# Linear attention and a SiLU feed-forward: reordered loads, split exps and a later transpose around batch 1 of 8

## The chip, the cores and the metric

The kernel runs on one core of a Trainium2 chip. A core has five engines with queues of their own, each working in program order: PE (TensorE, matmuls and transposes), DVE (VectorE), ACT (ScalarE), POOL (GpSimd) and SP (SyncE, which here only issues transfers). Sixteen DMA engines move data between the main memory (HBM) and the on-chip memory (SBUF); matmul results stand in PSUM, eight banks in all. The metric is the device time of one execution in microseconds (us); lower is better.

## The reference

Attention without a softmax over pairs of rows, then a feed-forward layer, in float32:

```python
# q, k, v: (8 batches, 8 heads, 576 rows, 64)
q_s = exp(q - max(q, -1)); q_s /= sum(q_s, -1) + 1e-9
k_s = exp(k - max(k, 2));  k_s /= sum(k_s, 2) + 1e-9
kv   = einsum('bhsd,bhse->bhde', k_s, v)
attn = einsum('bhsd,bhde->bhse', q_s, kv)
# x: (4608 tokens, 512), heads side by side
h = x @ w_in                 # 512 -> 2048
out = (h * sigmoid(h)) @ w_out   # 2048 -> 512
```

## The kernel before

There are two tilings at once. The attention goes by batch b (8 of 576 rows), the feed-forward by chunk t (9 of 512 tokens); a chunk's tokens come from one or two batches. Chunk 0 is done 576 wide, so that it takes the whole of batch 0.

For a batch, q, k and v are loaded in two halves of four heads each (`load`, index cc; two buffers of each name, so a load waits until the same half of the batch before has been read). `exp_q` and `exp_k` run on ACT. The row sums of q come from `qsum` (DVE) or, for batch 1, from `qsum_pair` (two additions on POOL) and `qsum_end` (DVE); `qnorm` divides. `tr` transposes q on PE and `trcopy` brings it out of PSUM (batches 0 and 1), or `q_transpose` does both by a DMA (later batches). `vcast` rounds v to bf16 in the one buffer `vaug`, which has a column of constants beside v, `kv_both` multiplies k and v on PE (72 small matmuls, and `kvcopy` on DVE, which divides by the sums of k), and `xt` makes the chunk's input XT.

The feed-forward of the later chunks is done with Winograd's form of Strassen's method: seven products in place of eight, over sums and differences of blocks. `ws_op`, `xs_op`, `t_op` and `s_op` make those sums on DVE, all from SBUF to SBUF: WS from W1, XS from XT, T1 to T4 from W2, and S from the activations. `group` is a product of the first layer with its evacuation (`group_snap`, `group_add`, `group_silu`), `prod` one of the second. Chunk 0 uses plain matmuls: `wide` (first layer, 16 units, each with a tanh on ACT and a product on DVE, in three pairs of PSUM banks in turn) and `mm2_plain` (second layer).

The order is written out by hand. `units` is the list of PE's pieces of work; `plan(u, f)` issues f just before unit u, and functions with the same u go out in the order of the plans. Each engine does what it is given in that order, so a plan sets an instruction's place in the queues of ACT, DVE, POOL and SP, and not a time. `b1 = begin[1]` is 16, the first unit after the wide ones: nine units of `mm2_plain`, then fourteen that alternate `group` of chunk 1 with `mm2_plain`, then eight plain units of chunk 1; `begin[2]` is 47.

What the change touches: the issue order of the loads on POOL's queue ahead of the main loop (lines 561 to 573); the plans at units 9 to 13 for batch 1's exps and sums; `tr(1, 1, ...)` and its `trcopy` (lines 777 and 779); `ws_op(1, 0)` (line 801); and batch 3's six loads, issued by SP among the stores of chunk 0 (`mm2_plain_out` ends in `store`, two transfers on SP's queue).

Of the kernel before, what the change touches and what calls it, by code (L numbers as in the profile page):

```python
# [17 lines left out]
def kernel(  # L18
# [9 lines left out]
    nc = tc.nc  # L28
# [4 lines left out]
    J = S // P  # L33
# [53 lines left out]
    def copy(eng, o, i):  # L87
        if eng is nc.scalar:
            eng.copy(out=o, in_=i)  # L89
        else:  # L90
            eng.tensor_copy(o, i)  # L91

    def load(b, name, src, cc, eng):
        t = ld.tile([128, 2, J * D], FP32, name=name)
        st[b][name, cc] = t
        x = src[b].rearrange("(g r) (p j) d -> g (r p) (j d)", r=2, j=J)
        eng.dma_start(out=t, in_=x.rearrange("g x y -> x g y")[:, 2 * cc:2 * cc + 2, :])  # L97

    def jgd(b, name, cc):
        return st[b][name, cc].rearrange("p g (j d) -> p j g d", d=D)  # L100

    def half(t, cc):
        return t[:, :, cc * 128:(cc + 1) * 128].rearrange("p j (g d) -> p j g d", d=D)

    def exp_q(b, cc, g0=0, g1=2):
        if "eq" not in st[b]:
            st[b]["eq"] = ap.tile([128, J, NG * D], BF16, name="eq")
        nc.scalar.activation(  # L108
            out=half(st[b]["eq"], cc)[:, :, g0:g1], in_=jgd(b, "qt", cc)[:, :, g0:g1], func=ACT.Exp
        )  # L110
# [4 lines left out]
    def vcast(b, cc, eng, g0=0, g1=2):  # L115
        o = vaug[:, :, 2 * cc + g0:2 * cc + g1, 0:D]
        i = jgd(b, "vt", cc)[:, :, g0:g1, :]
        copy(eng, o, i)

    def qsum_pair(b, cc):  # L120
        e = half(st[b]["eq"], cc)
        t1 = mp.tile([128, 2 * TCH], FP32, name="h0", bufs=1)[:, 0:J * D]
        t1 = t1.rearrange("p (j g d) -> p j g d", g=2, d=D // 2)
        t2 = mp.tile([128, 2 * TCH], FP32, name=f"h{cc + 1}", bufs=1)[:, 0:J * D // 2]
        t2 = t2.rearrange("p (j g d) -> p j g d", g=2, d=D // 4)
        nc.gpsimd.tensor_tensor(
            out=t1, in0=e[:, :, :, 0:D // 2], in1=e[:, :, :, D // 2:D], op=ALU.add
        )
        nc.gpsimd.tensor_tensor(
            out=t2, in0=t1[:, :, :, 0:D // 4], in1=t1[:, :, :, D // 4:D // 2], op=ALU.add  # L130
        )
        st[b]["t2", cc] = t2

    def qsum_end(b, cc):
        new_zq(b)
        nc.vector.reduce_sum(out=st[b]["zq"][:, cc], in_=st[b]["t2", cc], axis=AX.X)
        nc.vector.reciprocal(out=st[b]["rzq"][:, cc], in_=st[b]["zq"][:, cc])
# [16 lines left out]
    def qnorm(b, cc, eng):  # L154
        e = half(st[b]["eq"], cc)
        r = st[b]["rzq"][:, cc]
        eng.tensor_tensor(  # L157
            out=e, in0=e, in1=r[:, :, :, None].to_broadcast([128, J, 2, D]), op=ALU.mult
        )

    def new_qt(b):
        if "qT" not in st[b]:
            st[b]["qT"] = ap.tile([128, J, 2, 128], BF16, name="qT", bufs=2)
        return st[b]["qT"]
# [7 lines left out]
    def tr(b, cc, j0, j1, bank):  # L172
        t = PS[:, bank, :].bitcast(BF16)
        for j in range(j0, j1):
            nc.tensor.transpose(
                out=t[:, (j - j0) * 128:(j - j0 + 1) * 128],
                in_=st[b]["eq"][:, j, cc * 128:(cc + 1) * 128],
                identity=ident,
            )

    def trcopy(b, cc, j0, j1, bank, eng=nc.vector):
        t = PS[:, bank, :].bitcast(BF16)[:, 0:(j1 - j0) * 128].rearrange("x (j y) -> x j y", y=128)
        copy(eng, new_qt(b)[:, j0:j1, cc, :], t)
# [25 lines left out]
    def kv_both(b):  # L209
        kv(b, 0)  # L210
        kv(b, 1)
        kvcopy(b)
# [92 lines left out]
    def wa(c, f):  # L305
        return W1[:, 2 * c:2 * c + 2, f * 128:(f + 4) * 128]
# [4 lines left out]
    def ws_op(i, g):  # L311
        w, f0, f1 = WS[g], 4 * g + 8, 4 * g
        in0, in1, op = {
            1: (wa(0, f1), wa(1, f1), ALU.add),
            2: (w[0], wa(0, f0), ALU.subtract),
            3: (wa(0, f0), wa(0, f1), ALU.subtract),
            4: (wa(1, f0), w[1], ALU.subtract),
        }[i]
        nc.vector.tensor_tensor(out=w[i - 1], in0=in0, in1=in1, op=op)
# [30 lines left out]
    def group_silu(t, i, f, n):  # L350
        x = group_bank(t, False) if i is None else four(t, i)
        nc.scalar.activation(out=group_out(t, f, n), in_=x, func=ACT.Silu, scale=1.0 / XS)  # L352
# [46 lines left out]
    def store(t, col, o):  # L399
        for i in range(2):  # L400
            nc.sync.dma_start(out=rows(t, col + i * P), in_=o[i * P:(i + 1) * P, :])
# [11 lines left out]
    def mm2_plain_out(t, m, eng):  # L413
        if m % 2 == 0:
            st[t]["ow"] = mp.tile([128, 2, DM], FP32, name="ow", bufs=3)
        o = st[t]["ow"][:, m % 2]
        if eng is nc.scalar:
            nc.scalar.activation(out=o, in_=PS[:, 2 + m], func=ACT.Copy, scale=OS)
        else:
            nc.vector.tensor_scalar_mul(out=o, in0=PS[:, 2 + m], scalar1=OS)  # L420
        store(t, m * 128, o)
# [22 lines left out]
    def t_op(i, eng, f0=0, f1=HF):  # L444
        o, in0, in1 = {
            1: (T1, B12, B11),
            2: (T2, B22, T1),
            3: (T3, B22, B12),
            4: (T4, B21, T2),
        }[i]  # L450
        f = slice(f0, f1)
        eng.tensor_tensor(out=o[:, f], in0=in0[:, f], in1=in1[:, f], op=ALU.subtract)  # L452
# [97 lines left out]
    def load_w2(f0, f1):  # L550
        nc.gpsimd.dma_start(
            out=W2[:, f0:f1, :],
            in_=w_out[f0 * 128:f1 * 128, :].rearrange("(fc p) o -> p fc o", p=128),
        )
# [10 lines left out]
    load_w1(8, 16, 2, 4)  # L565
    load(1, "qt", q, 0, nc.gpsimd)
    load(1, "qt", q, 1, nc.gpsimd)
    load(1, "kt", k, 0, nc.gpsimd)
    load(1, "kt", k, 1, nc.gpsimd)
    load_w2(0, 4)  # L570
    load_w2(4, 8)
    load(1, "vt", v, 0, nc.gpsimd)
    load(1, "vt", v, 1, nc.gpsimd)
# [39 lines left out]
    def plan(u, f):  # L613
        at.setdefault(u, []).append(f)
# [141 lines left out]
    for i in (1, 2, 6, 5, 7, 4, 3):  # L756
# [3 lines left out]

    b1 = begin[1]

    plan(9, lambda: (load_w2(8, 12), exp_q(1, 0), qsum_pair(1, 0)))
    plan(12, lambda: (exp_q(1, 1, 0, 1), qsum_end(1, 0), qnorm(1, 0, nc.gpsimd)))
    plan(12, lambda: load(2, "qt", q, 0, nc.gpsimd))
    plan(13, lambda: (exp_q(1, 1, 1, 2), qsum_pair(1, 1)))
# [7 lines left out]
    plan(b1 + 3, lambda: (load(2, "kt", k, 0, nc.gpsimd), load(2, "kt", k, 1, nc.gpsimd)))  # L774
    plan(b1 + 6, lambda: (load(2, "vt", v, 0, nc.gpsimd), load(2, "vt", v, 1, nc.gpsimd)))
    plan(b1 + 4, lambda: vcast(1, 0, nc.scalar))
    plan(b1 + 5, lambda: (tr(1, 1, 0, 5, 0), tr(1, 1, 5, J, 1)))
    plan(b1 + 5, lambda: (vcast(1, 1, nc.scalar, 0, 1), vcast(1, 1, nc.vector, 1, 2)))
    plan(b1 + 6, lambda: (trcopy(1, 1, 0, 5, 0, nc.scalar), trcopy(1, 1, 5, J, 1)))
    plan(b1 + 7, lambda: kv_both(1))  # L780
    plan(b1 + 8, lambda: xt(1, 0))
    plan(b1 + 9, lambda: xt(1, 1))
# [11 lines left out]
    plan(b1 + 17, lambda: (vcast(2, 0, nc.gpsimd), vcast(2, 1, nc.gpsimd)))  # L794
    plan(b1 + 22, lambda: (group_silu(1, 2, 4, 1), group_silu(1, 0, 12, 0)))
    plan(b1 + 18, lambda: t_op(1, nc.vector))
    plan(b1 + 23, lambda: mm2_plain_out(0, 0, nc.scalar))
    plan(b1 + 23, lambda: (load(3, "qt", q, 0, nc.sync), load(3, "kt", k, 1, nc.sync)))
    plan(b1 + 23, lambda: mm2_plain_out(0, 1, nc.vector))
    plan(b1 + 24, lambda: group_silu(1, 1, 12, 1))  # L800
    plan(b1 + 24, lambda: (ws_op(1, 0), ws_op(2, 0)))
    plan(b1 + 24, lambda: [load(3, x, y, i, nc.sync) for x, y, i in (
        ("vt", v, 0), ("vt", v, 1), ("kt", k, 0), ("qt", q, 1)
    )])
    plan(b1 + 25, lambda: kv_both(2))
    plan(b1 + 26, lambda: t_op(2, nc.vector))
    plan(b1 + 27, lambda: xt(2, 0, nc.vector))
# [42 lines left out]
```

The softmax here doesn't subtract the row's maximum and nothing guards it: scores larger than these inputs give would overflow.

## Time and profile before

| | us |
|---|---|
| median of 6 runs | 263.88 (263.82 to 264.1) |
| the profiled execution | 263.95 |
| its span in the trace | 262.2 |
| PE busy | 252.8 |
| DVE busy | 208.3 |
| ACT busy | 186.5 |
| POOL busy | 67.8 |

The span runs from the first to the last instruction of the trace; the time also holds what lies around it. Busy time is the union of an engine's instructions. A timeline's line has the start in us, the time in us, the engine and line, the operation, out<-in with the shapes, and how many instructions are merged (x2); in brackets stands the idle time of the engine before it and what ended that. The rows for DMA issues have transfers of 576 KB each for q, k and v:

```profile
out_dram<-ow SPq DMA_DIRECT2D x64, 128.0 KB, 2.4
qt<-in_q_dram SPq DMA_DIRECT2D x12, 576.0 KB, 4.8
kt<-in_k_dram SPq DMA_DIRECT2D x12, 576.0 KB, 5.8
vt<-in_v_dram SPq DMA_DIRECT2D x12, 576.0 KB, 5.5
```

The last column is the median from issue to landing.

### The profile page before, as it was taken

The page shows a single profiled execution, that of the slowest core. Times are in us where ns is not written, and L with a number is a line of the kernel's source. Part 1 is how long each engine was busy: PE and PEld are TensorE (multiplying, and loading weights), DVE is VectorE, ACT ScalarE, POOL GpSimd, SP SyncE. Part 2 cuts the span into 40 slices and gives each one's busy share as a digit, 9 for nine tenths or more (in the row PEclk, how much of TensorE's full clock was granted, in tenths as well). Part 3 has the DMA queues.
Part 4 walks back from the last instruction along what each step waited for, and adds up shares of the span by engine and source line. Part 5 has one row for each costly group of instructions (what it writes and reads, how often), then busy time and mean ns, then how long its engine had stood idle before and what let it go on. Part 6 is the DMA issues. An engine that isn't in the chain of part 4 may idle for free.

```text
span 262.2 us, 6406 instructions
## 1 busy us (share of the span) xinstructions
PE 252.8 (96%) x2732; PEld 203.2 (78%) x2732; DVE 208.3 (79%) x268; ACT 186.5 (71%) x210; POOL 67.8 (26%) x63
## 2 busy tenths in 40 slices
PE   8899999999899999999999999999999999999993
PEld 3458645656788888888888888888888888888882
DVE  2867777799997999799979997999798448855932
ACT  4766874898796699669966997699664757584610
POOL 1753792550460306030603060306000000000004
PEclk9999999999999999999999999999999999999999
DMA  6999999669987488748774889550525002500534
GB/s 242 335 198 327 263 320 331 254 126 311 401 321 180 136 207 272 162 155 205 277 181 138 209 270 134 187 115 0 93 52 111 2 0 47 116 2 1 119 83 120
DMA packets 35453, 45.89 MB, mean 175 GB/s; under 512 B 16209, under 2 KB 19985, under 8 KB 35425
## 3 DMA queue, kind: packets, MB, share of 16 engines
q1 hardware_dynamic: 29488, 33.63, 46.8%
q0 software_dynamic: 5616, 11.60, 16.9%
q8 instruction: 21, 0.34, 0.5%
q10 hardware_dynamic: 320, 0.26, 0.4%
q14 instruction: 8, 0.06, 0.1%
HBM read 36.70 MB, written 9.44 MB: 176 GB/s over the span
## 4 chain that ended last, share of the span: by engine, by line
PE 76%; DVE 12%; DMA 4%; issue 2%; POOL 2%; ACT 2%; SPq 1%; POOLq 0%; DVEq 0%; ACTq 0%
PE PS L468 33%; PE PS L368 31%; PE PS L405 4%; DMA vt<-in_v_dram 4%; PE PS L258 3%; PE PS L189 2%; PE PS L228 2%; DVE h L346 2%; DVE S L442 1%; DVE GT L251 1%; DVE zq L148 1%; SPq L97 1%; DVE GT L442 1%; DVE T L452 1%; POOL out_dram L730 1%
## 5 line engine op out<-in xcount | busy, mean ns | idle before, releaser
L346 DVE TENSOR_TENSOR h<-PS,h 128x1024 f32<-128x1024 f32 (+1 forms) x45 | 54.0, 1200 | 12.0 <-PE PS L368 6.0
L468 PEld LDWEIGHTS <-GT 128*128 128x128 f16 x512 | 49.6, 98 | 6.9 <-issue 1.2
L368 PEld LDWEIGHTS <-WS 128*128 128x128 f16 x480 | 46.8, 98 | 7.0 <-issue 1.0
L468 PE MATMUL PS<-W,GT 128*128 128x256 f16 x384 | 49.1, 273 | 0.0
L368 PE MATMUL PS<-XS,WS 128*128 128x256 f16 (+1 forms) x360 | 46.3, 272 | 0.2
L352 ACT ACTIVATE GT<-h 128x1024 f16<-128x1024 f32 (+1 forms) x45 | 46.1, 1047 | 0.3 <-DVE h L346 0.3
L89 ACT COPY h<-PS 128x1024 f32<-128x1024 f32 (+1 forms) x35 | 35.1, 1002 | 13.2 <-PE PS L368 12.5
L157 POOL TENSOR_TENSOR eq<-eq,rzq 128x1152 bf16<-128x1152 bf16 x13 | 27.5, 2116 | 57.9 <-DVE rzq L152 53.9
L468 PEld LDWEIGHTS <-S 128*128 128x128 f16 x384 | 37.1, 98 | 6.2 <-issue 1.0
L368 PEld LDWEIGHTS <-W 128*128 128x128 f16 x360 | 34.7, 98 | 4.8 <-issue 0.5
L468 PE MATMUL PS<-T,S 128*128 128x256 f16 x256 | 32.7, 273 | 0.7 <-DVE S L442 0.7
L368 PE MATMUL PS<-XT,W 128*128 128x256 f16 (+1 forms) x240 | 29.5, 272 | 0.1
L352 ACT ACTIVATE GT<-PS 128x1024 f16<-128x1024 f32 (+1 forms) x15 | 15.2, 1016 | 18.9 <-PE PS L368 18.9
L91 POOL CAST vaug<-vt 128x1152 bf16<-128x1152 f32 x12 | 15.4, 1290 | 44.6 <-DMA vt<-in_v_dram 33.3
L730 POOL DMA_DIRECT2D out_dram<-ow x5 | 2.7, 545 | 72.1 <-DVE ow L715 72.1
L108 ACT ACTIVATE eq<-qt 128x1152 bf16<-128x1152 f32 (+1 forms) x17 | 18.8, 1107 | 2.7 <-DMA qt<-in_q_dram 2.7
L113 ACT ACTIVATE ek<-kt 128x1152 bf16<-128x1152 f32 x16 | 18.4, 1155 | 2.6 <-DMA kt<-in_k_dram 2.6
L148 DVE TENSOR_REDUCE zq<-eq 128x18 f32<-128x1152 bf16 x12 | 16.1, 1345 | 3.8 <-ACT eq L108 3.8
L258 PE MATMUL PS<-XT,W 128*128 128x288 f16 x128 | 16.3, 286 | 0.5 <-DVE XT L91 0.2
L468 PE MATMUL PS<-W,S 128*128 128x256 f16 x128 | 16.5, 273 | 0.0
L488 DVE SCALAR_TENSOR_TENSOR ow<-PS,sc 128x512 f32<-128x512 f32 x7 | 4.8, 691 | 14.4 <-ACT sc L484 14.4
L251 DVE SCALAR_TENSOR_TENSOR GT<-sg,PS 128x576 f16<-128x576 f32 x16 | 11.8, 753 | 5.0 <-ACT sg L250 4.9
(78 smaller groups left out, 348.5 us busy)
## 6 DMA issues: line engine op xcount, KB each, us to landing
out_dram<-ow SPq DMA_DIRECT2D x64, 128.0 KB, 2.4
qt<-in_q_dram SPq DMA_DIRECT2D x12, 576.0 KB, 4.8
kt<-in_k_dram SPq DMA_DIRECT2D x12, 576.0 KB, 5.8
vt<-in_v_dram SPq DMA_DIRECT2D x12, 576.0 KB, 5.5
qt<-in_q_dram POOLq DMA_DIRECT2D x4, 576.0 KB, 11.1
kt<-in_k_dram POOLq DMA_DIRECT2D x4, 576.0 KB, 12.1
vt<-in_v_dram POOLq DMA_DIRECT2D x4, 576.0 KB, 12.2
W<-in_moe_w_out_dram POOLq DMA_DIRECT2D x4, 512.0 KB, 15.1
```

Source lines behind the costliest of these rows:

```text
L89: eng.copy(out=o, in_=i)
L91: eng.tensor_copy(o, i)
L108: nc.scalar.activation(out=half(st[b]["eq"], cc)[:, :, g0:g1], in_=jgd(b, "qt", cc)[:, :, g0:g1], func=ACT.Exp)
L113: nc.scalar.activation(out=half(ek, cc), in_=jgd(b, "kt", cc), func=ACT.Exp)
L148: nc.vector.reduce_sum(out=z, in_=e, axis=AX.X)
L157: eng.tensor_tensor(out=e, in0=e, in1=r[:, :, :, None].to_broadcast([128, J, 2, D]), op=ALU.mult)
L251: nc.vector.scalar_tensor_tensor(out=o, in0=s, scalar=1.0, in1=i, op0=ALU.add, op1=ALU.mult)
L258: nc.tensor.matmul(out=PS[:, 2 * (fb % 3) + n, 0:S // 2], lhsT=W1[:, c, fb * 128:(fb + 1) * 128], rhs=XTS[0][:, c, n * (S // 2):(n + 1) * ...
L346: nc.vector.tensor_tensor(out=four(t, i), in0=group_bank(t, True), in1=four(t, i), op=ALU.add)
L352: nc.scalar.activation(out=group_out(t, f, n), in_=x, func=ACT.Silu, scale=1.0 / XS)
L368: nc.tensor.matmul(out=PS[:, bank + p // 2, (p % 2) * HT:(p % 2) * HT + width(t)], lhsT=a[:, c, p * 128:(p + 1) * 128], rhs=bb[:, c, 0:wid ...
L468: nc.tensor.matmul(out=PS[:, bank, m * HN:(m + 1) * HN], lhsT=a[:, fc, m * 128:(m + 1) * 128], rhs=bb[:, fc, :], start=(first and fc == 0) ...
```

## The change

Five edits, all of order:

- the first quarter of W2 is loaded before batch 1's two halves of k instead of after them;
- `exp_q(1, 0)` is split into two exps of two heads each, one at unit 9 and one at unit 10, and `qsum_pair(1, 0)` goes with the second to unit 10;
- `tr(1, 1, ...)` and its `trcopy` go one unit later;
- `ws_op(1, 0)` goes from b1+24 to b1+13; `ws_op(2, 0)` stays;
- batch 3's six loads, which SP issued partly between the stores of chunk 0's first two output blocks and partly after them, are all issued before those stores, and in another order: q's first half, both of v, both of k, q's second half.

```diff
     load(1, "qt", q, 1, nc.gpsimd)
+    load_w2(0, 4)
     load(1, "kt", k, 0, nc.gpsimd)
     load(1, "kt", k, 1, nc.gpsimd)
-    load_w2(0, 4)
     load_w2(4, 8)
...
-    plan(9, lambda: (load_w2(8, 12), exp_q(1, 0), qsum_pair(1, 0)))
+    plan(9, lambda: (load_w2(8, 12), exp_q(1, 0, 0, 1)))
+    plan(10, lambda: (exp_q(1, 0, 1, 2), qsum_pair(1, 0)))
...
-    plan(b1 + 5, lambda: (tr(1, 1, 0, 5, 0), tr(1, 1, 5, J, 1)))
+    plan(b1 + 6, lambda: (tr(1, 1, 0, 5, 0), tr(1, 1, 5, J, 1)))
...
-    plan(b1 + 6, lambda: (trcopy(1, 1, 0, 5, 0, nc.scalar), trcopy(1, 1, 5, J, 1)))
+    plan(b1 + 7, lambda: (trcopy(1, 1, 0, 5, 0, nc.scalar), trcopy(1, 1, 5, J, 1)))
...
+    plan(b1 + 23, lambda: [load(3, x, y, i, nc.sync) for x, y, i in (
+        ("qt", q, 0), ("vt", v, 0), ("vt", v, 1), ("kt", k, 1), ("kt", k, 0), ("qt", q, 1)
+    )])
     plan(b1 + 23, lambda: mm2_plain_out(0, 0, nc.scalar))
-    plan(b1 + 23, lambda: (load(3, "qt", q, 0, nc.sync), load(3, "kt", k, 1, nc.sync)))
     plan(b1 + 23, lambda: mm2_plain_out(0, 1, nc.vector))
     plan(b1 + 24, lambda: group_silu(1, 1, 12, 1))
-    plan(b1 + 24, lambda: (ws_op(1, 0), ws_op(2, 0)))
-    plan(b1 + 24, lambda: [load(3, x, y, i, nc.sync) for x, y, i in (
-        ("vt", v, 0), ("vt", v, 1), ("kt", k, 0), ("qt", q, 1)
-    )])
+    plan(b1 + 13, lambda: ws_op(1, 0))
+    plan(b1 + 24, lambda: ws_op(2, 0))
```

## The prediction

> **What bounds the kernel now.** I read the page's busy shares first, then the chain of waits, then the timelines of POOL, DVE, PE and SP from 20 to 90 us.
>
> ```profile
> PE 252.8 (96%) x2732; PEld 203.2 (78%) x2732; DVE 208.3 (79%) x268; ACT 186.5 (71%) x210; POOL 67.8 (26%) x63
> PE 76%; DVE 12%; DMA 4%; issue 2%; POOL 2%; ACT 2%; SPq 1%; POOLq 0%; DVEq 0%; ACTq 0%
> ```
>
> PE is busy 96%, so little can be gained: what is not PE in the chain. In order of time the chain runs on PE alone from 82 us; before that it goes through POOL (32.9 to 35.1), DVE (35.9 to 37.4), PE, and DVE again without a break from 58.3 to 81.8. By windows, the stage from 62.9 has PE 25.75 busy of 26.7, the three later ones 26.20 of 26.20. So the change can act only before 82 us, and everything after follows unaltered.
>
> Two DVE stretches decide. The first hangs on GpSimd's row sums of batch 1:
>
> ```profile
> 26.67 1.28 POOL L126 TENSOR_TENSOR h<-eq 128x576 f32<-128x576 bf16 x1 [0.43 <-ACT eq L108]
> 28.04 0.80 POOL L129 TENSOR_TENSOR h<-h 128x288 f32<-128x288 f32 x1
> 30.07 2.12 POOL L157 TENSOR_TENSOR eq<-eq,rzq 128x1152 bf16<-128x1152 bf16 x1 [1.24 <-DVE rzq L137]
> ...
> 35.11 0.45 DVE L136 TENSOR_REDUCE zq<-h 128x18 f32<-128x288 f32 x1 [1.59 <-POOL h L129]
> ...
> 39.52 0.75 DVE L91 CAST vaug<-vt 128x576 bf16<-128x576 f32 x1
> ...
> 39.90 0.90 PE L189 MATMUL PS<-vaug,ek 64*64 64x65 bf16 x72
> ```
>
> The reader is to see that DVE waits 1.59 for GpSimd, and then (no idle is printed until the L91 cast of v, which ends at 40.27) is DVE's queue full. kv(1) on PE (L189, 72 matmuls) takes 0.90, where the same row takes 0.81 at 56.73 and 0.80 at 77.28: PE waited some 0.1 in its middle, for that cast. From there to 57.5 PE is full.
>
> The second stretch is DVE from kvcopy(2) at 57.71 on, and here GpSimd and DVE get in each other's way:
>
> ```profile
> 52.28 1.84 DVE L452 TENSOR_TENSOR T<-W 128x2048 f16<-128x2048 f16 x1
> 58.33 1.22 DVE L452 TENSOR_TENSOR T<-W,T 128x2048 f16<-128x2048 f16 x1
> 60.69 1.22 DVE L452 TENSOR_TENSOR T<-W,T 128x2048 f16<-128x2048 f16 x1
> 61.82 0.69 DVE L319 TENSOR_TENSOR WS<-W 128x1024 f16<-128x1024 f16 x1
> 62.42 0.69 DVE L319 TENSOR_TENSOR WS<-W,WS 128x1024 f16<-128x1024 f16 x1
> 69.88 1.99 DVE L442 TENSOR_TENSOR S<-S,GT 128x2048 f16<-128x2048 f16 x1
> ...
> 52.99 3.25 POOL L91 CAST vaug<-vt 128x1152 bf16<-128x1152 f32 x2
> 67.54 1.16 POOL L91 CAST vaug<-vt 128x1152 bf16<-128x1152 f32 x1 [11.30 <-PE PS L468]
> 69.05 1.75 POOL L91 CAST vaug<-vt 128x1152 bf16<-128x1152 f32 x1 [0.35 <-DMA vt<-in_v_dram]
> ```
>
> A DVE tensor_tensor whose inputs both lie in SBUF and a GpSimd operation don't run together: T1 takes 1.84 while GpSimd's L157 runs until 53.05, T2 takes 1.22 alone; the second cast of batch 3 takes 1.75 under s_op(1), the first 1.16 beside DVE operations on PSUM; then s_op(2) takes 1.99, as it waits until that cast ends at 70.80. PE's largest wait (0.7, for DVE S L442) is for this s_op(2).
>
> **The change, part by part.**
>
> W2's first rows ahead of k. The two k loads (issued 13.85 and 15.03) land after 14.4 and 14.6 us, at 28.2 and 29.7; W2's first block (16.07, 16.1 us) at 32.1. So a k takes 1.46 and this block 2.4 of the queue. Put first, the block lands at 28.2-1.46+2.4 = 29.2 and the k at 30.6 and 32.1. POOL's other loads keep their places and bytes ahead. exp_k(1) runs at 34.11 and 35.18 on ACT, so 3 us cover the delay; without that cover exp_k would be up to 2.4 late. PE's L405 at 32.17, whose weight load waited 0.43 for W2, starts up to 0.28 earlier (the 32 matmuls from 27.97 need 4 times 0.98, the step of the tanhs at 20.97 and 21.95, so 31.89).
>
> Exps in halves. exp_q(1,0) at 25.43 takes 1.16 on ACT; a half takes 0.68, and the next instruction starts 0.58 later (29.69 to 30.27). So: first half 25.43, the tanh of block 9 at 26.01 rather than 26.49, second half 26.55 to 27.23. The wide matmuls lose a wait of 0.1 to 0.18 at 27.97. But qsum_pair(1,0) is now issued after the second half: 27.23 instead of 26.59, **0.64 later**; L126 and L129 end at 29.48 instead of 28.84. On DVE qsum_end(1,0) stands behind the silu of block 11, which ends at 29.26 either way, and ran at 29.18. It now runs at 29.51: 0.33 later. Behind it on DVE stands the silu of block 12 (PE's block 15 starts 0.1 late, which the W2 gain covers). GpSimd waits for this reciprocal (1.24 idle before 30.07), so its qnorm, the load issue at 32.13, and qsum_pair(1,1) all come **0.33 later**, and so do DVE's 35.11 and everything behind it up to the cast at 40.27, now 40.60. Bounds 0.2 to 0.45 (ACT's step may be 0.1 off).
>
> Transposes a block on. tr(1,1) waited on PE for qnorm(1,1): the 16 L405 from 33.55 take 3.46 (1.73 for 8 in the chain of waits), so to 37.0, and it starts at 37.58, 0.57 later. A block later (0.87) the wait is about 0.2. But kv(1) behind it waits for the DVE cast all the same: PE comes to it some 0.5 to 0.9 earlier and waits that much longer. Net of the W2 and transpose edits: at most the 0.1 that kv(1) now loses; I take 0 and the 0.33 remains. trcopy(1,1) moves behind the cast that it already stood behind. From kv(1) to kv(2) PE is full, so the 0.33 arrives at DVE's kvcopy(2).
>
> ws_op(1,0) earlier. It costs 0.72 at 56.06, just before the 0.20 for which DVE waits for kv(2). Taking it away there only lengthens that wait: gain 0. In its new place it falls into the 0.85 in which DVE waits for ACT's exp_q(2,1) before 49.07. It starts before GpSimd's L157 (48.41) and pushes it by some 0.4, and the next L157 waits for DVE anyway. Cost 0; if the order were the other way, up to 0.6.
>
> Batch 3's loads ahead of the stores. On SP the transpose ends at 55.84; the first store issues at 56.72, and the v loads at 60.40 and 61.03, behind four stores, landing after 7.0 us. Now six loads go out from 56.2 (with the 0.33), one each 0.5, and the four stores from about 59.3, 2.6 late; their buffers are next written after 74 us, so nobody waits. What do the loads give? ACT's 1.36 wait for k at 70.42 goes, worth 0, since DVE shows no wait for ACT there. What counts is when GpSimd **casts v**. At 81.75 two v loads follow a transpose just so:
>
> ```profile
> 81.75 1.11 SPq L97 DMA_DIRECT2D vt<-in_v_dram  x2
> 85.97 1.16 POOL L91 CAST vaug<-vt 128x1152 bf16<-128x1152 f32 x1 [7.05 <-DMA vt<-in_v_dram]
> 87.51 1.16 POOL L91 CAST vaug<-vt 128x1152 bf16<-128x1152 f32 x1 [0.38 <-DMA vt<-in_v_dram]
> ```
>
> 4.2 from issue to cast, 1.54 to the next. With q first, the casts are ready at 56.2+4.2+1.5 = 61.9 and 63.5 instead of 67.54 and 69.05. They leave s_op(2): S1 and S2 take 2.48 together in the next stage (95.39 to 97.87) against 3.31 here, **-0.83**. They meet T4, WS3, WS4 (60.69 to 63.11, plus 0.33), then the XS operations and T3 until 66.4; only the 0.69 of L420 from PSUM lies between. DVE has no idle here. The price from both sides: if each cast gets in between two of these, each costs at least the 0.83 seen at s_op(2) and at most about 0.97 (cast 1.03 once it has the port, less overlap), so 1.66 to 1.95. If DVE keeps the port as long as it has such work, the first cast waits for L420 and delays XS by the 0.43 by which it outlasts L420, the second nothing: 0.43. If they met nothing: 0. I take 1.8, as at 53.05 and 69.77 the waiting engine got its turn as soon as the other's instruction ended, though more was queued.
>
> The Trainium skill, "SBUF — State Buffer", section "Who interferes with whom", says that with two SBUF inputs DVE shares a read port with GpSimd and that whoever issues first holds it for the whole instruction, and its summary advises scheduling around the critical path. No row shows DVE's operations back to back with a cast waiting; by the rule the cast that waits since 61.9 was there before WS3, which gives the upper price, a sum of +1.45 and 265.3, where the lower price gives +1.16 and 265.0; it speaks against these loads.
>
> **Sum:** +0.33 (row sums) - 0.83 (s_op(2)) + 1.8 (casts) = +1.3. The profiled execution took 263.95 (span 262.2), 0.07 above the median 263.88: 263.88+1.3 = **265.2**. Its own range: +0.2-0.83+1.66 = +1.0 to +0.45-0.83+1.95 = +1.6: 264.9 to 265.5.
>
> **Rivals.**
>
> 1. DVE keeps the port. +0.33-0.83+0.43 = -0.1: 263.8, up to 264.3 if one cast slips in at the semaphore gap before XS2 (64.04 to 64.14) but costs half. For it: DVE starts each operation some 0.08 before the last ends. Against: the hand-over at 53.05.
>
> 2. Faster: the casts meet nothing. They would have to wait until DVE's PSUM operations L346 and L91 (from 66.6), or the loads land as late as before. -0.83+0.33 = -0.5, and with the row sums' delay absorbed -0.83: 263.05 to 263.4. It decides if the v loads land after 66 us. For it: six loads of 576 KB share the engines with a transpose. Against: 81.75.
>
> 3. PE's waits count in full: kv(1) is not tied to DVE, so 0.28+0.57 come off and, with ws_op(1,0) gone, DVE passes it on: -0.85, with the casts' +1.0 264.0, without any 262.2. Against: the 0.90 of L189.
>
> **How the numbers follow.** Forecast 0.62, rival 1 0.12, rival 2 0.13, rival 3 0.08 (half of it faster), more than 266 (ws_op(1,0) in the wrong order too, +0.6) 0.05. What a measurement tells from no change is about 0.2%, 0.53 us. Slower: 0.62+0.05+0.04 of rival 1 = 0.71; same: 0.08+0.04 = 0.12; faster: 0.13+0.04 = 0.17. The range 263.7 to 265.9 leaves out rival 2, rival 3's faster half and the case above 266.
>
> **What would show it.** L129's first end near 29.5; the cast of v on DVE ending near 40.6 and L189 of kv(1) well over 0.9; batch 3's casts on POOL near 62 and 64, some over 1.16; WS or XS rows over a microsecond; s_op(2) at 1.2; PE's wait for S L442 nearly gone, with longer waits at L368 near 68. I am wrong if the casts land elsewhere or WS and XS keep their 0.69 and 0.42.

## The result and the profile after

| | median us | runs | ratio to before, 95% interval |
|---|---|---|---|
| before, same chip | 264.09 | 37 | |
| changed | 264.79 | 17 | 1.0025 (1.0016 to 1.0035) |

The changed kernel is slower by 0.66 us by the ratio, 0.42 to 0.92 by its interval. Forecast was +1.3, with a range of 263.7 to 265.9. The profiled execution took 265.12, with a span of 263.4 against 262.2.

The page of the changed kernel, busy shares and the chain by engine:

```profile
PE 253.3 (96%) x2732; PEld 203.1 (77%) x2732; DVE 208.7 (79%) x268; ACT 186.8 (71%) x211; POOL 68.2 (26%) x63
PE 72%; DVE 10%; issue 5%; DMA 5%; POOL 4%; ACT 1%; POOLq 0%; DVEq 0%; ACTq 0%
```

Nothing stands out there: busy times moved by 0.5 us at most. The answer lies in the timelines. First GpSimd's row sums, on POOL's timeline:

```profile
27.63 1.28 POOL L126 TENSOR_TENSOR h<-eq 128x576 f32<-128x576 bf16 x1 [0.85 <-ACT eq L108]
28.99 0.80 POOL L129 TENSOR_TENSOR h<-h 128x288 f32<-128x288 f32 x1
30.72 2.12 POOL L157 TENSOR_TENSOR eq<-eq,rzq 128x1152 bf16<-128x1152 bf16 x1 [0.93 <-DVE rzq L137]
...
62.70 3.02 POOL L91 CAST vaug<-vt 128x1152 bf16<-128x1152 f32 x2 [5.82 <-DMA vt<-in_v_dram]
```

L129 ends at 29.79 instead of 28.84 and qnorm starts at 30.72 instead of 30.07. Counted from the first wide matmul (15.52 before, 15.39 here), qnorm comes 0.78 later. Some 0.45 of this belongs to this execution and not to the change: a weight load waited for W1, which it did not do in the profile before, and the first 120 wide matmuls take 15.66, where they take 15.21 in two versions below (`ws_back`, `w2_back`); there qnorm comes 0.33 later than before. From the waits of the weight loads:

```profile
PEld L258 <- DMA W<-in_moe_w_in_dram: 0.4, 1, 0.4
```

PE's timeline shows what became of the wait that the transposes lost. Before:

```profile
15.52 12.27 PE L258 MATMUL PS<-XT,W 128*128 128x288 f16 x96 [0.25 <-DVE XT L91]
...
37.58 0.66 PE L175 MATMUL PS<-ident,eq 128*128 128x128 bf16 x9 [0.42 <-DVE eq L157]
...
71.92 1.05 PE L468 MATMUL PS<-T,S 128*128 128x256 f16 x8 [0.71 <-DVE S L442]
```

and after:

```profile
15.39 15.66 PE L258 MATMUL PS<-XT,W 128*128 128x288 f16 x120 [0.25 <-DVE XT L91]
...
38.23 0.66 PE L175 MATMUL PS<-ident,eq 128*128 128x128 bf16 x9 [0.16 <-DVE eq L157]
38.73 1.03 PE L405 MATMUL PS<-W,GT 128*128 128x512 f16 x4
39.68 0.50 PE L189 MATMUL PS<-vaug,ek 64*64 64x65 bf16 x37
40.97 0.48 PE L189 MATMUL PS<-vaug,ek 64*64 64x65 bf16 x35 [0.79 <-DVE vaug L91]
...
66.58 1.05 PE L368 MATMUL PS<-XS,WS 128*128 128x256 f16 x8 [0.24 <-DVE XS L329]
...
69.52 1.03 PE L368 MATMUL PS<-XS,WS 128*128 128x256 f16 x8 [1.02 <-DVE h L346]
...
73.11 1.05 PE L468 MATMUL PS<-T,S 128*128 128x256 f16 x8
```

The 0.42 idle before the second transposes is 0.16, W2 is no longer waited for, and kv(1) is now split in two: after 37 of its 72 matmuls PE waits 0.79 for DVE's cast of v. At 66.58 and 69.52 there are waits of 0.24 and 1.02 that the profile before did not have; the wait of 0.71 for s_op(2) is gone. DVE's timeline from T4 on shows why; first the row of XS1 before, then the changed kernel:

```profile
63.62 0.42 DVE L329 TENSOR_TENSOR XS<-XT 128x512 f16<-128x512 f16 x1
```

```profile
61.33 1.22 DVE L452 TENSOR_TENSOR T<-W,T 128x2048 f16<-128x2048 f16 x1
62.46 0.69 DVE L319 TENSOR_TENSOR WS<-W 128x1024 f16<-128x1024 f16 x1
63.06 1.64 DVE L319 TENSOR_TENSOR WS<-W,WS 128x1024 f16<-128x1024 f16 x1
64.62 0.68 DVE L420 TENSOR_SCALAR ow<-PS 128x512 f32<-128x512 f32 x1
65.23 0.77 DVE L329 TENSOR_TENSOR XS<-XT 128x512 f16<-128x512 f16 x1
66.10 0.43 DVE L329 TENSOR_TENSOR XS<-XT,XS 128x512 f16<-128x512 f16 x1
...
71.83 1.23 DVE L442 TENSOR_TENSOR S<-S,GT 128x2048 f16<-128x2048 f16 x1
```

WS4 takes 1.64 in place of 0.69 and XS1 0.77 in place of 0.42: **+1.30** together. s_op(2) takes 1.23 in place of 1.99: **-0.76**. The two casts stand right beside: they begin at 62.70 and run with hardly a gap until 65.72.

A distance tells the kernels of this study apart better than the whole time, in which single runs of one kernel scatter by about 1 us: from the first wide matmul (L258) to the first product that reads S2 (L468, T and S). That product starts right behind s_op(2). In the profiles the distance is 71.92-15.52 = 56.40 before and 73.11-15.39 = 57.72 after, +1.32. Of this 15.66-15.21 = 0.45 is the wait for W1, which leaves 57.27, +0.87 (`w2_back` and `ws_back`, whose times are those of the changed kernel, have 57.28 and 57.37). Each distance is that of a single profile.

### The profile page after: what moved, and what is told of

It reads as the page before. It is cut to its first block, busy times and chain, and to the rows that moved or that the text cites. A ratio compares the mean times of both kernels' runs of the same rounds, so it can differ in the third digit from the quotient of the medians.

```text
span 263.4 us, 6411 instructions
## 1 busy us (share of the span) xinstructions
PE 253.3 (96%) x2732; PEld 203.1 (77%) x2732; DVE 208.7 (79%) x268; ACT 186.8 (71%) x211; POOL 68.2 (26%) x63
## 4 chain that ended last, share of the span: by engine, by line
PE 72%; DVE 10%; issue 5%; DMA 5%; POOL 4%; ACT 1%; POOLq 0%; DVEq 0%; ACTq 0%
PE PS L468 33%; PE PS L368 31%; DMA qt<-in_q_dram 5%; PE PS L405 3%; PE PS L228 2%; DVE h L346 2%; PE PS L189 2%; DVE WS L319 2%; POOL W L545 1%; PE PS L276 1%; POOL h L126 1%; DVE zq L148 1%; DVE S L442 1%; DVE GT L442 1%; POOL out_dram L730 1%
## 5 line engine op out<-in xcount | busy, mean ns | idle before, releaser
L468 PEld LDWEIGHTS <-GT 128*128 128x128 f16 x512 | 49.6, 98 | 6.9 <-issue 1.2
L468 PE MATMUL PS<-W,GT 128*128 128x256 f16 x384 | 49.1, 273 | 0.0
L468 PEld LDWEIGHTS <-S 128*128 128x128 f16 x384 | 37.1, 98 | 5.4 <-issue 1.0
L368 PEld LDWEIGHTS <-W 128*128 128x128 f16 x360 | 34.7, 98 | 4.8 <-issue 0.5
L468 PE MATMUL PS<-T,S 128*128 128x256 f16 x256 | 32.7, 273 | 0.0
L258 PE MATMUL PS<-XT,W 128*128 128x288 f16 x128 | 16.7, 286 | 0.6 <-DVE XT L91 0.2
L468 PE MATMUL PS<-W,S 128*128 128x256 f16 x128 | 16.5, 273 | 0.0
L258 PEld LDWEIGHTS <-W 128*128 128x128 f16 x128 | 12.3, 97 | 4.9 <-issue 1.5
```

The costliest lines, as they stand in the source:

```text
L258: nc.tensor.matmul(out=PS[:, 2 * (fb % 3) + n, 0:S // 2], lhsT=W1[:, c, fb * 128:(fb + 1) * 128], rhs=XTS[0][:, c, n * (S // 2):(n + 1) * ...
L368: nc.tensor.matmul(out=PS[:, bank + p // 2, (p % 2) * HT:(p % 2) * HT + width(t)], lhsT=a[:, c, p * 128:(p + 1) * 128], rhs=bb[:, c, 0:wid ...
L468: nc.tensor.matmul(out=PS[:, bank, m * HN:(m + 1) * HN], lhsT=a[:, fc, m * 128:(m + 1) * 128], rhs=bb[:, fc, :], start=(first and fc == 0) ...
```

## The experiments

All were timed against the kernel before on the same chip; the versions ran on three chips. The last column is that distance.

| kernel | median, before beside it | ratio, 95% interval | distance |
|---|---|---|---|
| before | | 1 | 56.40 |
| changed | 264.79, 264.09 | 1.0025 (1.0016 to 1.0035) | 57.72 |
| loads_only | 264.30, 263.93 | 1.0013 (1.0001 to 1.0026) | 56.96 |
| all_but_loads | 264.36, 263.93 | 1.0009 (0.9997 to 1.0022) | 56.73 |
| whole_exp | 264.52, 263.93 | 1.0019 (1.0006 to 1.0033) | 56.95 |
| cast_gate | 263.44, 263.93 | 0.9978 (0.9965 to 0.9991) | 56.06 |
| cast_first | 263.79, 263.90 | 0.9992 (0.9980 to 1.0005) | 56.58 |
| first_gate | 262.70, 263.90 | 0.9947 (0.9927 to 0.9968) | 55.59 |
| first_gate_whole | 262.62, 263.90 | 0.9945 (0.9924 to 0.9966) | 55.06 |
| ws_back | 264.75, 263.90 | 1.0028 (1.0014 to 1.0042) | 57.37 |
| w2_back | 264.85, 264.14 | 1.0023 (1.0014 to 1.0032) | 57.28 |
| fgw_w2_back | 262.69, 264.14 | 0.9940 (0.9927 to 0.9953) | 55.33 |
| fgw_tr_back | 263.03, 264.14 | 0.9954 (0.9941 to 0.9967) | 55.66 |

### The loads alone, and everything else alone

`loads_only` is the kernel before with the new list of loads at b1+23; `all_but_loads` is the changed kernel with the old ones.

```diff
+    plan(b1 + 23, lambda: [load(3, x, y, i, nc.sync) for x, y, i in (
+        ("qt", q, 0), ("vt", v, 0), ("vt", v, 1), ("kt", k, 1), ("kt", k, 0), ("qt", q, 1)
+    )])
     plan(b1 + 23, lambda: mm2_plain_out(0, 0, nc.scalar))
-    plan(b1 + 23, lambda: (load(3, "qt", q, 0, nc.sync), load(3, "kt", k, 1, nc.sync)))
...
-    plan(b1 + 24, lambda: [load(3, x, y, i, nc.sync) for x, y, i in (
-        ("vt", v, 0), ("vt", v, 1), ("kt", k, 0), ("qt", q, 1)
-    )])
```

> The kernel before with only the batch-3 loads moved. Theory A (GpSimd's casts of v come earlier and alternate with DVE's SBUF operations): WS4 about 1.6 and XS1 about 0.8 in place of 0.69 and 0.42, s_op(2) 1.2 in place of 2.0, so +1.3 - 0.8 = about +0.5 us against before. Theory B (the loads are harmless and the loss is made before kv(1)): 0, or a gain up to 0.8.

> The changed kernel with the batch-3 loads back where they were. Theory A: only the later row sums are left, +0.3 us against before; qsum_end(1,1) some 0.3 later, kv(1) on PE split by a wait of 0.8 to 0.9 for the DVE cast, s_op(2) again about 2.0. Theory B: the whole +0.7 stays.

DVE's timeline in loads_only:

```profile
62.40 1.64 DVE L319 TENSOR_TENSOR WS<-W,WS 128x1024 f16<-128x1024 f16 x1
...
64.56 0.77 DVE L329 TENSOR_TENSOR XS<-XT 128x512 f16<-128x512 f16 x1
...
71.17 1.23 DVE L442 TENSOR_TENSOR S<-S,GT 128x2048 f16<-128x2048 f16 x1
```

and in all_but_loads:

```profile
63.00 0.69 DVE L319 TENSOR_TENSOR WS<-W,WS 128x1024 f16<-128x1024 f16 x1
64.20 0.42 DVE L329 TENSOR_TENSOR XS<-XT 128x512 f16<-128x512 f16 x1
...
70.46 1.99 DVE L442 TENSOR_TENSOR S<-S,GT 128x2048 f16<-128x2048 f16 x1
```

The long WS4 and XS1 go with the loads and nothing else; the long s_op(2) goes with the old loads. The distances grow by 0.56 and 0.33, as expected (+0.5 and +0.3), together 0.89 against the +0.87 above, and the two ratios' excesses, 0.0013 and 0.0009, add up to 0.0022 of the 0.0025. Theory B falls: the loads are not harmless. Taken by itself all_but_loads is not told from before by its time; its +0.33 rests on the trace.

### Holding GpSimd's casts back

In `cast_gate` the loads stay as changed, and one GpSimd copy of one element of T3 stands before batch 3's casts in POOL's queue, so that they start only after DVE's T3:

```diff
     plan(begin[2] + 1, lambda: t_op(3, nc.vector))
+    plan(begin[2] + 1, lambda: nc.gpsimd.tensor_copy(gate, T3[0:1, 0, 0:1]))
```

> The changed kernel with one more GpSimd copy of a single element of T3 ahead of batch 3's casts, which holds them back until DVE's T3 is done; loads as changed. Theory A: WS4 0.69 and XS1 0.42 again, the casts run under L346 and L91, which read PSUM, and touch s_op(1) by at most 0.3: about 1.0 to 1.3 us faster than the changed kernel, 0.3 to 0.6 faster than before. Theory B: no difference from the changed kernel.

POOL's timeline in cast_gate:

```profile
66.77 0.18 POOL L815 CAST gate<-W 1x1 f32<-1x1 f16 x1 [10.19 <-DVE W L452]
66.89 2.24 POOL L91 CAST vaug<-vt 128x1152 bf16<-128x1152 f32 x2
```

and DVE's:

```profile
62.76 0.68 DVE L319 TENSOR_TENSOR WS<-W,WS 128x1024 f16<-128x1024 f16 x1
...
63.96 0.41 DVE L329 TENSOR_TENSOR XS<-XT 128x512 f16<-128x512 f16 x1
...
66.63 1.21 DVE L346 TENSOR_TENSOR h<-PS,h 128x1024 f32<-128x1024 f32 x1
67.76 1.21 DVE L91 COPY h<-PS 128x1024 f32<-128x1024 f32 x1
68.89 1.32 DVE L442 TENSOR_TENSOR S<-GT 128x2048 f16<-128x2048 f16 x1
70.32 1.22 DVE L442 TENSOR_TENSOR S<-S,GT 128x2048 f16<-128x2048 f16 x1
```

The two casts take 2.24 where they took 3.02, under two DVE operations that read PSUM and keep their 1.21; only s_op(1) loses 0.1. With the same loads, the same casts and one instruction more, the kernel is 0.0047 faster than the changed one (0.9978 against 1.0025, about 1.2 us) and clearly faster than before. WS4 and XS1 are back at 0.68 and 0.41 although the loads' transfers are as in the changed kernel. So it is *when* the casts run that costs, and not the loads as such.

### The row sums

`whole_exp` takes the split of the exp back:

```diff
-    plan(9, lambda: (load_w2(8, 12), exp_q(1, 0, 0, 1)))
-    plan(10, lambda: (exp_q(1, 0, 1, 2), qsum_pair(1, 0)))
+    plan(9, lambda: (load_w2(8, 12), exp_q(1, 0), qsum_pair(1, 0)))
```

> The changed kernel with exp_q(1,0) whole at unit 9 again, its row sums with it. Theory A: the row sums end 0.6 earlier, GpSimd's chain and the DVE cast before kv(1) 0.33 earlier, 0.3 us faster than the changed kernel. Rival: the exps' place sets nothing, same as the changed kernel.

L129 ends at 28.92 again and the wait inside kv(1) falls from 0.79 to 0.52, on PE's timeline:

```profile
39.38 0.50 PE L189 MATMUL PS<-vaug,ek 64*64 64x65 bf16 x37
40.40 0.48 PE L189 MATMUL PS<-vaug,ek 64*64 64x65 bf16 x35 [0.52 <-DVE vaug L91]
```

The distance is 56.95, 0.32 shorter than the changed kernel's 57.27. The split buys nothing in the wide stage itself: with the whole exp PE waits 0.18 ahead of its last four units, with the halves 0.19 ahead of its last one, and the wide matmuls take 16.53 from start to end in both (whole_exp and ws_back). The times (1.0019 against 1.0025) do not resolve 0.3 us, so by time alone this one is open; the trace agrees with theory A.

### What holds kv(1)

`cast_first` puts DVE's cast of v in front of ws_op(1,1) and ws_op(2,1), in the queue where it stood behind them:

```diff
-    plan(b1 + 5, lambda: (vcast(1, 1, nc.scalar, 0, 1), vcast(1, 1, nc.vector, 1, 2)))
+    plan(b1 + 5, lambda: vcast(1, 1, nc.scalar, 0, 1))
+    plan(b1 + 2, lambda: vcast(1, 1, nc.vector, 1, 2))
```

> The changed kernel with DVE's cast of v for kv(1) put ahead of ws_op(1,1) and ws_op(2,1) in DVE's queue. Theory A (the W2 and transpose edits were given back because kv(1) waits for this cast): PE's wait of 0.8 inside L189 goes, kvcopy(1) comes some 0.9 earlier and stays so until kv(2); 0.7 to 0.9 us faster than the changed kernel, about level with before or 0.2 faster. Rival (PE waits for something else there): same as the changed kernel.

PE's timeline in cast_first:

```profile
39.10 0.81 PE L189 MATMUL PS<-vaug,ek 64*64 64x65 bf16 x72
```

kv(1) is in one piece. The ratio falls from 1.0025 to 0.9992, 0.87 us: the gain that the W2 and transpose edits had made, and that PE had given back a few units later, now arrives. By the distance it is 57.27-56.58 = 0.69.

### Both together, and the rest

`first_gate` has both repairs, `first_gate_whole` the whole exp as well.

> Both repairs: the DVE cast ahead of ws_op, and GpSimd's casts of batch 3 held until T3 is done. Theory A: the gains add, -0.9 and -1.2 from the changed kernel: about 262.6, 0.5% faster than before. Rival: the second DVE stretch swallows the earlier kv(2), so no more than the held casts alone gave (0.9978).

> As first_gate, with exp_q(1,0) whole at unit 9. Theory A: with the cast out of the way PE waits for qnorm(1,1) at tr(1,1), 0.16 there in the changed kernel; the row sums 0.33 earlier take that wait: 0 to 0.2 us faster than first_gate. Rival (the halves save PE waits in the wide stage): 0.1 slower.

The gains add: 0.9947 and 0.9945, by the ratios **1.4 us faster than before** and 2.1 faster than the changed kernel. The whole exp shortens the distance by 0.53, more than the expected 0 to 0.2; but first_gate's profile has the wait for W1 again (120 wide matmuls in 15.67, 0.46 more than 15.21) and first_gate_whole's does not. Without it 0.07 is left, too little for these two profiles to tell, and the times do not tell it either.

`ws_back` and `w2_back` take one edit each out of the changed kernel:

> The changed kernel with ws_op(1,0) back at b1+24. Theory A: DVE's idle time before kvcopy(2) falls from 0.8 to about 0.1 and kvcopy(2) starts at most 0.1 later; the first GpSimd product of batch 2 takes 2.12 in place of 2.33; 0 to +0.1 us. Rival: the moved sum is what keeps DVE free, and 0.5 or more is lost.

> The changed kernel with W2's first rows behind k again. Theory A: kv(1) waits for the DVE cast anyway, so 0.0 us against the changed kernel (at most 0.1). Rival (the wait for W2 is on the path): 0.2 to 0.3 slower.

Both are the changed kernel within the interval (1.0028 and 1.0023). In ws_back DVE no longer waits ahead of kvcopy(2). DVE's rows of kvcopy(2) in the changed kernel, then of kvcopy(2) and XS1 in ws_back:

```profile
58.24 0.18 DVE L200 RECIPROCAL rz<-PS 128x4 f32<-128x4 f32 x1 [0.81 <-PE PS L189]
...
57.81 0.18 DVE L200 RECIPROCAL rz<-PS 128x4 f32<-128x4 f32 x1
...
64.80 0.87 DVE L329 TENSOR_TENSOR XS<-XT 128x512 f16<-128x512 f16 x1
```

Its distance is 0.1 longer than 57.27, and this 0.1 is XS1's 0.87 in place of 0.77: the second cast starts only at 64.24 here, half a microsecond after the first has ended. In w2_back PE waits 0.47 for W2 again; kv(1) waits 0.31 less, 0.48 instead of 0.79, and the 0.16 ahead of the second transposes is no longer printed, together 0.47:

```profile
32.49 1.04 PE L405 MATMUL PS<-W,GT 128*128 128x512 f16 x4 [0.47 <-DMA W<-in_moe_w_out_dram]
...
40.62 0.48 PE L189 MATMUL PS<-vaug,ek 64*64 64x65 bf16 x35 [0.48 <-DVE vaug L91]
```

That is a wait which changed its place. The last two ask whether these edits are worth something once nothing behind takes them back; both are first_gate_whole with one edit undone.

> The version with both repairs and the whole exp, with W2's first rows behind k again. Theory A: now nothing behind takes the gain back, so it is 0.2 to 0.3 us slower than with W2 ahead. Rival (W2 never mattered): the same.

> The version with both repairs and the whole exp, with the second transposes at b1+5 again. Theory A: PE waits 0.6 to 0.9 for qnorm(1,1) at them and nothing gives it back: 0.6 to 0.9 us slower than with them a block on. Rival: the same.

By the distance, yes: 0.27 longer without the W2 edit, 0.60 without the later transposes, one profile each. By the times it is unclear for W2 (0.9940 against 0.9945, intervals overlapping, another chip) and only leans that way for the transposes (0.9954).

## Why the prediction was right, and where its size was off

- **Only what lies ahead of 82 us counts.** From the product that reads S2 to the end of the span, both profiles take the same: 262.2-71.92 and 263.4-73.11, 190.3 each.
- **Row sums, +0.33.** all_but_loads has +0.33 in the distance. The prediction put L129's end at 29.48, 13.96 behind the first wide matmul (13.32 before); it was 13.94 to 13.96 in ws_back, w2_back and all_but_loads, and 14.40 in the profile after, which W1 held up. What the split was to save did not come: the wide stage's wait went from its last four units to its last one.
- **W2 and the transposes, 0.** Shown for W2 by w2_back, and for both together by cast_first: they saved waits of PE, and kv(1) waited longer for the cast. No run takes the transposes alone out of the changed kernel. Rival 3 (the waits count in full) falls for the changed kernel, and describes the version with the cast moved.
- **ws_op(1,0), 0.** Shown by ws_back, to 0.1.
- **s_op(2), -0.83.** It measured -0.76. The prediction took S1 and S2 together; 0.07 of its 0.83 is a gap between the two, 0.10 here and 0.03 in the stage that it compared with, and this gap is still 0.10 after the change (71.73 to 71.83).
- **The casts, +1.8: mis-sized.** They measured +1.30. The prediction had them ready at 61.9 and 63.5, one against WS3 and one against WS4, for at least 0.83 each. They came at 62.70 and 64.20. Some 0.3 of this delay moved DVE as well (W1) and changed nothing between the two. Against WS3 the casts were 0.5 late for two other reasons, seen in SP's timeline of the changed kernel:

```profile
53.72 2.77 SPq L167 DMA_TRANSPOSE qT<-eq  x1
56.67 0.44 SPq L97 DMA_DIRECT2D qt<-in_q_dram  x1
57.22 0.97 SPq L97 DMA_DIRECT2D vt<-in_v_dram  x2
```

  SP took 0.18 from the end of the transpose (56.49) to q, where none had been reckoned, and from q's issue to the first cast it was 6.03, reckoned as 5.7. loads_only, without the wait for W1, has the same two (0.19 and 6.07) and the same collisions. So WS3 had started, the first cast hit WS4 (+0.95, inside the 0.83 to 0.97), and most of the second ran beside L420, which reads PSUM; XS1 lost only +0.35. The prediction had named this shelter, the 0.69 of L420, and had counted on it for rival 1 only.
- **The sum.** With the measured terms it is +0.33 - 0.76 + 1.30 = +0.87, the +0.87 of the distance without W1's wait, and inside the 0.42 to 0.92 of the times. The forecast of +1.3 was twice the 0.66 of the ratio, and both values lie below the +1.0 to +1.6 that the prediction gave its own mechanism; the wider range, which makes room for rival 1, holds the time. The direction and the mechanism hold. Rival 1 falls with WS4's 1.64: DVE did not keep the port. Rival 2 falls by loads_only and by the 62.70 of the casts, and cast_gate is what it described: the casts meet (almost) nothing, and the kernel is faster.

WS4 stood in DVE's queue directly behind WS3 while the cast was already waiting, and it took 1.64 instead of 0.69: the port changes hands even between two DVE instructions that follow each other at once. The Trainium skill, "SBUF — State Buffer", section "Who interferes with whom", says that the first to issue has the port for the whole instruction. The run agrees: the cast is on record from 62.70, ahead of WS4 at 63.06, and WS4 is the one that lasts longer. This is the row that the prediction had missed.

## What to carry to other kernels

A wait that is removed is worth only what the next wait on the same queue leaves of it: look for the next wait behind it that is nearly due, here a cast that kv(1) already waited 0.1 for, because it stood behind 1.9 us of other DVE work. Data that arrive earlier also start their consumers earlier; when the consumer shares a port with the engine that bounds the stage, hold it back (one tiny instruction that depends on the right thing is enough) until that engine works from PSUM. And of five edits made together, two can be worth something and be hidden by one wait behind them.

## What was not expected of the hardware

- A GpSimd operation that met a DVE sum just before it lost less than the sum lasted: qnorm(2,0) took 2.33 beside the moved ws_op(1,0), 2.12 without it, where some 0.4 had been reckoned.
- When W1 lands differs from one execution to the next with the same code ahead of it: GpSimd's wait for it at W2's second block ends 3.4 to 3.8 behind the first wide matmul in seven profiles, and 4.1 and 4.4 behind it in the changed kernel's and first_gate's, and in these two a weight load of PE waits 0.4 for it. That is as large as most of the effects here, so two distances can be compared only when this wait is taken out of them.
